# Memory added in three parts, a minimum moved behind an eviction, and one memory piece a slot, in a two-branch attention kernel

## The chip, the cores and the metric

The kernel runs on one core of a Trainium2 chip. The metric is the device time of one execution in microseconds (us). The core's engines work side by side, each through its own queue in order: TensorE (PE) multiplies, VectorE (DVE) and ScalarE (ACT) read PE's results out of PSUM, GpSimd (POOL) applies masks, and SyncE (SP) issues nearly all DMAs.

## The reference

Two independent attention layers over the same shapes (2048 tokens, 640 columns, 32 heads of 20 columns); their outputs stand side by side in the result.

```python
# A: four chunks of 512 tokens, one after the other
phi = lambda t: jnp.where(t > 0, t + 1.0, jnp.exp(t))
for s in range(4):
    logits = einsum('bhqd,bhkd->bhqk', qs, ks) * scale + mask      # inside the chunk
    a_dot = einsum('bhqk,bhkd->bhqd', softmax(logits), vs)
    pq = phi(qs)
    a_mem = einsum('bhld,bhde->bhle', pq, M) / (einsum('bhld,bhd->bhl', pq, z)[..., None] + 1e-06)
    outs.append(g * a_mem + (1.0 - g) * a_dot)
    M = M + einsum('bhld,bhle->bhde', phi(ks), vs)
    z = z + sum over l of phi(ks)
A = concat(outs) @ wo
# B: causal attention in a sliding window of 256 tokens
B = softmax(scores inside the window) @ v @ wo
```

In A, `mask` is -1e9 where the key lies behind the query's position, so each chunk is causal. The first chunk finds an empty memory.

## The kernel before

**Stages.** The work is cut into eight stages in the order B0, A0, B1, A1, B2, A2, B3, A3: a branch and one of its four chunks of 512 tokens. A stage has eight units `g` of four heads (80 columns), and its score blocks are packed so that a pack fills 384 or 512 columns of PSUM. A pack is a **slot** (`self.slot`): B0 has slots 0 to 19, A0 20 to 39, B1 40 to 63, A1 64 to 83, B2 84 to 107, A2 108 to 127, B3 128 to 151, A3 152 to 171.

**What a slot issues**, in this order on every engine's queue (`body`, from L746): steps that an earlier slot put down for its start (`self.after`: `normalise`, and `spread`, the DMAs that bring the projected q or k into the layout for scores, tiles `qp` and `kp`); the scores of the pack (`scores`: PE writes two PSUM tiles `Sc`, ACT takes each with one exponential into `pt`, L495, POOL masks `pt`); steps put down for behind the scores (`self.behind`); if a unit is due, `weigh` (PE multiplies `pt` with v into a PSUM tile `D`, DVE evicts it as `oc`, L561, SP transposes it); `prefetch` (transposed loads `oT` of finished outputs); and then dense and memory pieces as `pick` chooses them.

**PSUM.** There are three `Sc` buffers and two `D` buffers. Every dense piece, memory piece and `weigh` takes a `D`, in the order of issue, and its first matmul waits until DVE has read the `D` two before it.

**Pieces.** A projection (`proj`, L291) is five matmuls and an eviction `qk` (L294), followed by a store; a projection of v (`vproj`, L351) and half an output tile (`out_half`, L630, eviction `ot` L633) are five matmuls of 320 columns. In A1, A2 and A3 there are memory pieces: eight `read`s (L465; three DVE operations, L472, L474, L475, write a part of the tile `omem`), two halves of the columns by four token tiles, the first half first, and behind them five `upd`s (L432, DVE L442, L443), which renew the memory; A3 has no `upd`. `pick` weighs all numbers of up to three dense, three memory and three output pieces against a budget for the slot.

**Feature map.** `phi` (L317) puts down two steps for a projection of A made in slot s. `exp`, behind the scores of s+1: DVE computes max(t+1, 1) (L333) and ACT exp(t) into `pe` (L335; two buffers). `rest`, behind the scores of s+2: DVE takes the minimum of both (L338), which waits for ACT, and for k SP issues a transpose (L342).

**Outputs.** `normalise` of a unit (L590) is a reciprocal and a product on DVE (L594, L599) into its 80 columns of the tile `otA` or `otB`. In A1 and A2 the last unit's `normalise` adds all 640 columns of `omem` for four token tiles in one DVE operation (L611, 128x2560); in A3 units 4 to 7 add, unit 4 the first 400 columns.

Of the kernel before, what the change touches and what calls it, by code (L numbers as in the profile page):

```python
# [14 lines left out]
D = 640  # L15
H = 32
DH = 20
G = 8
GW = 4 * DH
KT = 5  # L20
NC = 4
# [61 lines left out]
class Kern:  # L83

    def __init__(self, ctx, tc, ins, out2d):
        self.tc, self.nc = tc, tc.nc
        self.x = {"A": ins["A_x"][0], "B": ins["B_x"][0]}
        self.ins, self.out2d = ins, out2d
        ep = ctx.enter_context
        self.cp = ep(tc.tile_pool(name="consts", bufs=1))  # L90
        self.wp = ep(tc.tile_pool(name="weights", bufs=1))
        self.io = ep(tc.tile_pool(name="io", bufs=1))
        self.wk = ep(tc.tile_pool(name="work", bufs=1))
        self.dram = ep(tc.tile_pool(name="scratch", bufs=1, space=bass.MemoryType.DRAM))
        self.ps = ep(tc.tile_pool(name="ps", bufs=1, space=bass.MemoryType.PSUM))
        self.xT, self.qp, self.kp, self.o_tok = {}, {}, {}, {}
        self.omem, self.phiq, self.mz = None, None, {}
        self.slot = 0
        self.after, self.behind = {}, {}
        self.tiles = []  # L100
        self.ready = []

# [214 lines left out]
    def phi(self, c, which, m, t, st):  # L317

        nc = self.nc
        if (which == "q" and c == 0) or (which == "k" and c == NC - 1):  # L320
            return
        if which == "q":
            if m == 0:
                self.phiq = self.io.tile([P, CT, D], BF16, name="phiq", bufs=1)[:].rearrange(
                    "p t d -> p (t d)").rearrange("p (m s) -> p m s", m=KT)
            dst = self.phiq[:, m, :]
        else:
            pk = self.wk.tile([P, CH], BF16, name="phik", bufs=3)
            dst = pk[:]
        e = self.wk.tile([P, CH], BF16, name="pe", bufs=2)  # L330

        def exp():
            nc.vector.tensor_scalar(out=dst, in0=t[:], scalar1=1.0, scalar2=1.0,  # L333
                                    op0=ALU.add, op1=ALU.max)
            nc.scalar.activation(out=e[:], in_=t[:], func=ACT.Exp)  # L335

        def rest():
            nc.vector.tensor_tensor(out=dst, in0=dst, in1=e[:], op=ALU.min)  # L338
            if which == "k":
                if m == 0:  # L340
                    st["kt"] = self.wk.tile([P, KT, CT, P], BF16, name="pkt", bufs=1)
                nc.sync.dma_start_transpose(out=st["kt"][:, m, :, :], in_=pk[:])  # L342

        self.at_end(self.slot + 1, exp)
        self.at_end(self.slot + 2, rest)

    def vproj(self, br, c, tt, hf):
        nc = self.nc
# [241 lines left out]
    def normalise(self, u, tp):  # L590
# [7 lines left out]
        cols = slice(GW * u.g, GW * (u.g + 1))  # L598
# [2 lines left out]
                                in1=rr[:].unsqueeze(3).to_broadcast([P, CT, 4, DH]),  # L601
                                op=ALU.mult)
        if u.br == "A" and u.c > 0:
            if u.c < NC - 1:
                cols = slice(0, D if u.g == G - 1 else 0)
            elif u.g < G - 4:
                cols = slice(0, 0)
            elif u.g == G - 4:
                cols = slice(0, GW * (u.g + 1))
            if cols.stop > cols.start:  # L610
                nc.vector.tensor_tensor(out=o[:, :, cols], in0=o[:, :, cols],  # L611
                                        in1=self.omem[:, :, cols], op=ALU.add)
# [115 lines left out]
    def body(self):  # L728
# [4 lines left out]
        for n, ph in enumerate(phases):  # L733
            dense = lists[n]
            mem = []
            if ph.br == "A" and ph.c > 0:
                mem = [(0.4, lambda tt=tt, hf=hf: self.read(ph.c, tt, hf))
                       for hf in range(2) for tt in range(CT)] + upd[ph.c]
            outs = 2 * OUT_TILES[n]
# [5 lines left out]
            at = [0, 0, 0]  # L745
            for i, pk in enumerate(ph.packs):  # L746
# [15 lines left out]
                if self.ready and self.ready[0][0] <= self.slot:  # L762
                    self.weigh(self.ready.pop(0)[1])
                    done += 0.75
                if outs or i >= np_ - 3:
                    self.prefetch()
                part = sum(weights[:i + 1]) / sum(weights)
                can = 2 * sum(1 for t in self.turned if t[0] + 2 <= self.slot) + len(self.half)
# [5 lines left out]
                if due > room:  # L774
                    room, can = due, 0
                for kind in self.pick(part, room, dense[at[0]:at[0] + 3],
                                      mem[at[1]:at[1] + 3], min(outs - at[2], can, 3),
                                      at, (len(dense), len(mem), outs)):
                    if kind == 2:
                        done += 0.75  # L780
                        self.out_step()
                    else:
                        a = (dense, mem)[kind][at[kind]]
                        done += a[0]
                        a[1]()
                    at[kind] += 1
# [5 lines left out]
    def pick(self, part, room, dense, mem, outs, at, total):  # L792

        best = None
        for d in range(len(dense) + 1):
            for m in range(len(mem) + 1):
                for o in range(outs + 1):
                    cost = sum(a[0] for a in dense[:d] + mem[:m]) + 0.75 * o
                    off = abs(room - cost)
# [9 lines left out]
    def tail(self, br, c):  # L809
# [9 lines left out]
                                    op=ALU.mult)  # L819
        while self.turned or self.half:  # L820
            self.out_step()
        while self.after or self.behind:
            for f in self.after.pop(self.slot, []) + self.behind.pop(self.slot, []):
                f()
            self.slot += 1
        ps[0] = self.last_sc(0)
        self.last_mm(br, 0, 0, 3)
# [63 lines left out]
```

## Time and profile before

| | us |
|---|---|
| median of three runs | 381.29 |
| lowest and highest run | 380.61 and 384.25 |
| the profiled execution, whole | 378.70 |
| its span, first to last instruction | 376.8 |
| ACT busy in the span | 339.0 |
| PE busy in the span | 335.4 |
| POOL busy in the span | 253.1 |
| DVE busy in the span | 273.0 |

The profile is of one execution. In its rows "x" gives a number of instructions, and a bracket "[2.10 <-PE ...]" the idle time of the engine before the instruction and what ended it. A stretch in which ACT has no idle time runs at ACT's pace, whatever the other engines wait for in it.

### The profile page before, as it was taken

To read this page: it belongs to the slowest core of one execution; us is meant where nothing else is said; L and a number is where in the kernel's file an instruction comes from. 1 tells how busy PE (TensorE), PEld (TensorE's weight loads), DVE (VectorE), ACT (ScalarE), POOL (GpSimd) and SP (SyncE) were. 2 spreads that over 40 slices of the span, in tenths; PEclk is the share of its full clock that TensorE was granted. 3 is DMA by queue.
4 is the path that set the end of the run, shared out by engine and by line. 5 is a ranking of instruction groups with operands and counts; after the bars stand their busy time and mean duration, and the time that the engine had idled before them with its cause. 6 is when DMAs were issued, how large, how long until landed. Compare 5 with 4: busy or idle time off the path is not lost.

```text
span 376.8 us, 10338 instructions
## 1 busy us (share of the span) xinstructions
PE 335.4 (89%) x3930; PEld 159.9 (42%) x3930; DVE 273.0 (72%) x578; ACT 339.0 (90%) x385; POOL 253.1 (67%) x392
## 2 busy tenths in 40 slices
PE   7998898999887889899987898988999989998985
PEld 3433433433443334444433344444444435444443
DVE  2465776566887687888777885787877787778783
ACT  2678899999887999899997999988999999999982
POOL 9576685555784788455587888734568988955550
PEclk9999999999999999999998999999999999999999
DMA  8964466686454847729765949825765477544622
GB/s 253 314 220 131 115 155 149 123 209 144 117 119 125 177 115 136 204 79 132 110 154 144 154 115 134 168 72 119 127 117 123 108 157 134 120 100 98 116 69 71
DMA packets 112241, 52.07 MB, mean 138 GB/s; under 512 B 81856, under 2 KB 112192, under 8 KB 112192
## 3 DMA queue, kind: packets, MB, share of 16 engines
q1 hardware_dynamic: 112048, 51.33, 60.9%
q8 instruction: 31, 0.51, 0.6%
q14 instruction: 18, 0.15, 0.1%
q10 hardware_dynamic: 144, 0.08, 0.1%
HBM read 17.05 MB, written 15.07 MB: 85 GB/s over the span
## 4 chain that ended last, share of the span: by engine, by line
PE 42%; ACT 24%; DVE 18%; issue 7%; DMA 5%; POOL 2%; SPq 1%; ACTq 0%; DVEq 0%; POOLq 0%
ACT pt L495 22%; PE D L291 14%; PE Sc L489 7%; PE D L351 6%; PE D L544 4%; PE D L630 4%; DVE qk L294 4%; DVE oc L561 2%; PE D L253 2%; ACT pe L335 2%; DMA qpB<-qdB 2%; DVE omem L475 2%; PE D L273 2%; DMA ocT<-oc 2%; DMA omem<-in_B_x_dram 1%
## 5 line engine op out<-in xcount | busy, mean ns | idle before, releaser
L495 ACT ACTIVATE pt<-Sc 128x1024 bf16<-128x1024 f32 (+1 forms) x344 | 320.7, 1068 | 22.1 <-PE Sc L489 21.4
L509 POOL TENSOR_SCALAR_AFFINE_SELECT pt<-pt 128x512 bf16<-128x512 bf16 x254 | 168.5, 674 | 107.1 <-ACT pt L495 106.6
L515 POOL TENSOR_SCALAR_AFFINE_SELECT pt<-pt 128x512 bf16<-128x512 bf16 x112 | 79.0, 719 | 4.2 <-ACT pt L495 3.5
L294 DVE CAST qk<-D 128x512 bf16<-128x512 f32 x70 | 48.1, 688 | 30.4 <-PE D L291 28.9
L489 PE MATMUL Sc<-qpB,kpB 20*128 20x256 bf16 (+2 forms) x704 | 45.0, 277 | 7.6 <-ACT pt L495 5.9
L489 PE MATMUL Sc<-qpA,kpA 20*128 20x384 bf16 (+3 forms) x512 | 39.3, 300 | 4.0 <-ACT pt L495 3.7
L561 DVE CAST oc<-D 128x512 bf16<-128x512 f32 x46 | 31.6, 688 | 14.1 <-PE D L544 13.9
L630 PEld LDWEIGHTS <-oT 128*128 128x128 bf16 x280 | 25.1, 97 | 17.4 <-issue 6.3
L489 PEld LDWEIGHTS <-kpB 20*128 20x128 bf16 x704 | 14.2, 92 | 42.8 <-issue 41.3
L633 DVE CAST ot<-D 128x320 bf16<-128x320 f32 x56 | 26.8, 485 | 5.5 <-PE D L630 4.7
L291 PE MATMUL D<-xTA,Aq 128*128 128x512 bf16 x100 | 24.9, 380 | 5.1 <-DVE oc L561 4.2
L351 PE MATMUL D<-Av,xTA 128*128 128x320 bf16 x160 | 26.3, 300 | 2.5 <-DVE vA L359 1.8
L351 PE MATMUL D<-Bv,xTB 128*128 128x320 bf16 x160 | 25.6, 300 | 2.7 <-DVE phiq L576 2.1
L291 PE MATMUL D<-xTA,Ak 128*128 128x512 bf16 x100 | 26.1, 393 | 2.0 <-DVE qk L294 2.0
L544 PE MATMUL D<-pt,vB 128*32 128x384 bf16 (+2 forms) x720 | 26.3, 277 | 1.1 <-DVE ot L633 0.5
L630 PE MATMUL D<-Bo,oT 128*128 128x320 bf16 x160 | 26.3, 300 | 0.5 <-DVE omem L475 0.3
L544 PE MATMUL D<-pt,vA 128*32 128x256 bf16 (+3 forms) x576 | 23.6, 287 | 3.3 <-DVE qk L294 2.1
L489 PEld LDWEIGHTS <-kpA 20*128 20x128 bf16 x512 | 11.5, 91 | 28.0 <-issue 25.3
L630 PE MATMUL D<-Ao,oT 128*128 128x320 bf16 x120 | 20.2, 300 | 1.0 <-DVE omem L475 0.6
L359 DVE TENSOR_TENSOR vA<-D,omg 128x320 bf16<-128x320 f32 x32 | 15.2, 485 | 6.4 <-PE D L351 6.0
L291 PE MATMUL D<-xTB,Bk 128*128 128x512 bf16 x75 | 18.8, 381 | 1.2 <-DVE omem L475 0.8
L335 ACT ACTIVATE pe<-qk 128x512 bf16<-128x512 bf16 x30 | 19.5, 659 | 0.0
(102 smaller groups left out, 363.6 us busy)
## 6 DMA issues: line engine op xcount, KB each, us to landing
out_dram<-ot SPq DMA_DIRECT2D x31, 160.0 KB
kdA<-qk SPq DMA_DIRECT2D x20, 128.0 KB
qdA<-qk SPq DMA_DIRECT2D x20, 128.0 KB
kdB<-qk SPq DMA_DIRECT2D x17, 128.0 KB
qdB<-qk SPq DMA_DIRECT2D x17, 128.0 KB
kpB<-kdB SPq DMA_DIRECT2D x8, 160.0 KB
qpB<-qdB SPq DMA_DIRECT2D x8, 160.0 KB
kpA<-kdA SPq DMA_DIRECT2D x8, 160.0 KB
```

The lines of the kernel that those rows point to most:

```text
L291: nc.tensor.matmul(ps[:], lhsT=self.w[br + which][:, kt, m * P:(m + 1) * P], rhs=self.xT[br][:, kt, :], start=(kt == 0), stop=(kt == KT - 1))
L294: nc.vector.tensor_copy(out=t[:], in_=ps[:])
L335: nc.scalar.activation(out=e[:], in_=t[:], func=ACT.Exp)
L351: nc.tensor.matmul(ps[:, 0:320], lhsT=self.xT[br][:, kt, tt * P:(tt + 1) * P], rhs=self.w[br + "v"][:, kt, hf * 320:(hf + 1) * 320], start ...
L489: nc.tensor.matmul(ps[j // 2][:, j % 2, off * P:(off + nq) * P], lhsT=kp[rows, u.g, k0:k0 + P], rhs=self.qp[u.br][rows, u.g, q0 * P:(q0 + ...
L495: nc.scalar.activation(out=pt[:, 2 * hp:2 * hp + 2, 0:pk.used], in_=ps[hp][:, :, 0:pk.used], func=ACT.Exp, scale=SCALE)
L509: nc.gpsimd.affine_select(out=blk, in_=blk, pattern=[[0, 4], [1, P]], compare_op=ALU.is_ge, fill=0.0, base=0, channel_multiplier=-1)
L515: nc.gpsimd.affine_select(out=blk, in_=blk, pattern=[[0, 4], [-1, P]], compare_op=ALU.is_ge, fill=0.0, base=-1, channel_multiplier=1)
L544: nc.tensor.matmul(O[32 * j:32 * j + 32, q0 * P:(q0 + nq) * P], lhsT=v[:, kt % CT, v0:v0 + 32], rhs=pt[:, j, off * P:(off + nq) * P], star ...
L561: nc.vector.tensor_copy(out=oc[:], in_=O[:])
L630: nc.tensor.matmul(ps[:, 0:320], lhsT=st["oT"][:, m, :], rhs=self.w[br + "o"][:, m, hf * 320:(hf + 1) * 320], start=(m == 0), stop=(m == K ...
L633: nc.vector.tensor_copy(out=st["ot"][:, hf * 320:(hf + 1) * 320], in_=ps[:, 0:320])
```

## The change

Three edits. The minimum of the feature map (`rest`) goes into a list of its own, `last_of`, which is issued in the same slot s+2 but behind `weigh`; in a slot without a due unit it stands where it stood. In A1 and A2 the memory's part is added by the units 3 (320 columns), 5 (160) and 7 (160) in place of 640 columns by unit 7; A3 is as before. And `pick` is offered one memory piece and must take it as long as there is one, so that each slot of A1, A2 and A3 issues exactly one until they are used up; the dense and output pieces are then chosen around it.

```diff
-        self.at_end(self.slot + 2, rest)
+        self.last_of.setdefault(self.slot + 2, []).append(rest)
...
         if u.br == "A" and u.c > 0:
-            if u.c < NC - 1:
-                cols = slice(0, D if u.g == G - 1 else 0)
-            elif u.g < G - 4:
-                cols = slice(0, 0)
-            elif u.g == G - 4:
-                cols = slice(0, GW * (u.g + 1))
+            c0 = {3: 0, 5: 4, 7: 6}.get(u.g, u.g + 1)
+            if u.c == NC - 1:
+                c0 = 0 if u.g == G - 4 else u.g if u.g > G - 4 else u.g + 1
+            cols = slice(GW * c0, GW * (u.g + 1))
             if cols.stop > cols.start:
...
                     self.weigh(self.ready.pop(0)[1])
                     done += 0.75
+                for f in self.last_of.pop(self.slot, []):
+                    f()
...
-                                      mem[at[1]:at[1] + 3], min(outs - at[2], can, 3),
+                                      mem[at[1]:at[1] + 1], min(outs - at[2], can, 3),
...
         for d in range(len(dense) + 1):
-            for m in range(len(mem) + 1):
+            for m in [len(mem)]:
                 for o in range(outs + 1):
```

By the two programs, the numbers of instructions of each kind stay as they are but for four more additions on DVE. In A1 the last two q projections both fall into slot 77 (before: slots 76 and 77, the last of them first in slot 77), one half output tile moves from slot 83 to 73, and one v projection out of slot 78. In A2 the last two q projections both fall into slot 121 (before: 120 and 121), and a half output tile moves from slot 125 to 117. In A3 the eight reads fall into slots 152 to 159 (before: 152 to 163). Outside of these three stages the pieces of every slot are the same.

More of the change, by code (lines that the diff above doesn't have):

```diff
@@ L98, in __init__ @@
         self.slot = 0
[L99 removed]
+        self.after, self.behind, self.last_of = {}, {}, {}
         self.tiles = []
@@ L821, in tail @@
             self.out_step()
-        while self.after or self.behind:
-            for f in self.after.pop(self.slot, []) + self.behind.pop(self.slot, []):
-                f()
+        while self.after or self.behind or self.last_of:
+            for q in (self.after, self.behind, self.last_of):
+                for f in q.pop(self.slot, []):
+                    f()
             self.slot += 1
```

## The prediction

> **What bounds the kernel now.** I read the page's busy times first, then the stages as windows, then the waits, and last the timelines of the places where ACT stands still.
>
> ```profile
> PE 335.4 (89%) x3930; PEld 159.9 (42%) x3930; DVE 273.0 (72%) x578; ACT 339.0 (90%) x385; POOL 253.1 (67%) x392
> ACT pt L495 <- PE Sc L489: 21.4, 32, 2.1
> 55.10:92.90 37.80, 35.35 (x376) 14.61 (x375) 24.18 (x48) 37.80 (x43) 21.21 (x32) 1.00 0.68 155
> 92.90:147.60 54.70, 46.69 (x558) 22.93 (x557) 43.57 (x91) 49.97 (x59) 41.54 (x64) 1.00 0.54 132
> 147.60:187.60 40.00, 36.19 (x441) 18.00 (x440) 31.88 (x77) 37.80 (x41) 21.76 (x33) 1.00 0.70 130
> 187.60:239.60 52.00, 45.49 (x529) 20.86 (x529) 39.76 (x77) 49.46 (x59) 43.30 (x64) 0.97 0.71 138
> 239.60:281.00 41.40, 37.45 (x452) 18.85 (x451) 32.38 (x80) 37.56 (x42) 21.26 (x33) 1.00 0.62 123
> 328.40:365.90 37.50, 33.68 (x426) 17.49 (x427) 29.43 (x70) 37.02 (x41) 22.68 (x35) 1.00 0.44 100
> ```
>
> In a window row come the length, then the busy time of PE, weight loads, DVE, ACT and POOL, and the granted clock. The rows are A0, B1, A1, B2, A2 and A3. A0 runs without a gap in ACT: 37.80 us for 20 slots, 1.89 each. That is what the stages cost when ACT is never kept waiting, so an edit can win only what is idle in ACT's column: 4.73 in B1, 2.20 in A1, 2.54 in B2, 3.84 in A2, 0.48 in A3. The row of the waits says that ACT's exponentials waited 21.4 us for scores in all; PE brings them late, since it waits for a PSUM buffer `D` that DVE hasn't read yet. Each edit reorders DVE, so I look for what stands on DVE ahead of each late eviction.
>
> **Part 1, the addition.** B2's gap is nearly all one place, slots 89 to 91. The rows are DVE, PE, then ACT, and last the clock in a window of 3.4 us:
>
> ```profile
> 198.63 1.80 DVE L611 TENSOR_TENSOR otA<-otA,omem 128x2560 bf16<-128x2560 bf16 x1
> 200.36 0.84 DVE L338 TENSOR_TENSOR phik<-phik,pe 128x512 bf16<-128x512 bf16 x1
> 201.13 0.68 DVE L294 CAST qk<-D 128x512 bf16<-128x512 f32 x1
> 201.86 2.26 PE L291 MATMUL D<-xTA,Ak 128*128 128x512 bf16 x5 [2.01 <-DVE qk L294]
> 204.05 0.61 PE L489 MATMUL Sc<-qpB,kpB 20*128 20x384 bf16 x8
> 201.91 0.75 ACT L335 ACTIVATE pe<-qk 128x512 bf16<-128x512 bf16 x1
> 204.76 1.94 ACT L495 ACTIVATE pt<-Sc 128x1024 bf16<-128x1024 f32 x2 [2.10 <-PE Sc L489]
> 201.90:205.30 3.40, 3.40 (x25) 1.05 (x28) 1.67 (x5) 1.30 (x3) 2.78 (x5) 0.50 0.55 128
> L611 DVE TENSOR_TENSOR otA<-otA,omem 128x320 bf16<-128x320 bf16 x3 | 1.3, 428 | 0.1
> L611 DVE TENSOR_TENSOR otA<-otA,omem 128x1600 bf16<-128x1600 bf16 x1 | 1.0, 992 | 0.0
> ```
>
> The addition of 1.80 holds back a minimum and an eviction; PE idles 2.01, its next projection takes 2.26 at a granted clock of 0.50, and ACT idles 2.10. Afterwards unit 7 adds 640 elements a partition. On the line through the two forms (0.43 at 320, 0.99 at 1600) that is 0.57, so DVE is 1.2 ahead: the projection starts at 200.65. If the half clock goes with the long wait, it takes about 1.25 and the scores start near 201.85. ACT is busy until 201.91 + 0.75 = 202.66 anyway, so the whole **2.10** is won. If the half clock stays, the scores start at 202.84 and ACT, 0.71 behind as in the rows, at 203.55: 1.2 won.
>
> The Trainium skill (TensorE: Matmul & The Clock Gate, Part 1) puts the half clock behind at least one idle window of about 3.4 us, which speaks for the second figure. The trace disagrees: 0.50 follows an idle time of 2.01. By the page's rule the gain here would be 1.2 and the sum below 0.9 smaller.
>
> In A2 the same addition stands ahead of the first of the rows below. That gap is 0.58, below the 1.2 by which DVE is ahead: **0.55** won.
>
> ```profile
> 294.66 5.67 ACT L495 ACTIVATE pt<-Sc 128x1024 bf16<-128x1024 f32 x6 [0.58 <-PE Sc L489]
> 272.53 0.49 DVE L357 CAST vB<-D 128x320 bf16<-128x320 f32 x1
> 273.44 0.73 PE L544 MATMUL D<-pt,vA 128*32 128x256 bf16 x20
> ```
>
> What moves forward costs something. Unit 3 adds 1280 elements (0.85 on the line) in slots 79 and 123, which hold two v projections each. In slot 123 it pushes the eviction at 272.53 to 273.4, done 273.9; the `weigh` at 273.44 needs that buffer, so PE loses 0.5. ACT has no gap here and PE leads it by little: **-0.45** (from 0 to -0.7). In slot 79 a loss of that size lies in front of a larger one (part 3) and isn't counted again. Unit 5's 0.57 falls into slots 84 and 128, each with a single projection behind it: DVE's free time covers it; without that cover it would be 0.5 each.
>
> **Part 2, the minimum.** It matters where a unit is due in slot s+2 and ACT waits. That is B1's start, slots 47 and 50 (DVE, PE, ACT):
>
> ```profile
> 109.38 0.85 DVE L338 TENSOR_TENSOR phik<-phik,pe 128x512 bf16<-128x512 bf16 x1
> 110.15 0.68 DVE L561 CAST oc<-D 128x512 bf16<-128x512 f32 x1
> 116.13 0.49 DVE L338 TENSOR_TENSOR phiq<-phiq,pe 128x512 bf16<-128x512 bf16 x1 [0.69 <-ACT pe L335]
> 116.65 0.74 DVE L338 TENSOR_TENSOR phik<-phik,pe 128x512 bf16<-128x512 bf16 x1
> 117.31 0.72 DVE L333 TENSOR_SCALAR phiq<-qk 128x512 bf16<-128x512 bf16 x1
> 117.95 0.67 DVE L561 CAST oc<-D 128x512 bf16<-128x512 f32 x1
> 110.88 1.24 PE L291 MATMUL D<-xTA,Aq 128*128 128x512 bf16 x5 [0.91 <-DVE oc L561]
> 115.81 1.25 PE L291 MATMUL D<-xTA,Ak 128*128 128x512 bf16 x5
> 118.68 1.24 PE L291 MATMUL D<-xTA,Aq 128*128 128x512 bf16 x5 [1.61 <-DVE oc L561]
> 113.64 1.94 ACT L495 ACTIVATE pt<-Sc 128x1024 bf16<-128x1024 f32 x2 [1.62 <-PE Sc L489]
> 116.50 1.94 ACT L495 ACTIVATE pt<-Sc 128x1024 bf16<-128x1024 f32 x2
> 118.31 0.65 ACT L335 ACTIVATE pe<-qk 128x512 bf16<-128x512 bf16 x1
> 120.34 1.94 ACT L495 ACTIVATE pt<-Sc 128x1024 bf16<-128x1024 f32 x2 [1.38 <-PE Sc L489]
> ```
>
> In slot 47 the eviction `oc` moves ahead of a minimum of 0.85: PE's projection starts about 0.7 earlier. The output eviction behind it now stands behind the minimum, so the next projection gains only 0.5; the gap of 1.62 shrinks to 1.1. In slot 50 DVE idles 0.69 for ACT and then does two minima and L333 ahead of `oc`, while the unit's matmuls are done by 115.81. Afterwards L333 (0.72) and `oc` (0.67) go first: `oc` is done near 116.9, PE goes on at 117.06 instead of 118.68, and the 1.38 falls to some 0.2. Together 3.00 of gaps become 1.3: **1.7** (from 0.7, slot 47's half and a rest, to 2.5).
>
> A new wait comes with it: the exponential at 118.31 overwrites the `pe` buffer that the first minimum of slot 50 reads, and that minimum now waits for `oc`. Behind it on ACT's queue stand the exponentials of slot 51. The minimum would be done at 117.4, ACT arrives at 117.9 or later (113.64 less 0.5): it costs nothing, with 0.5 in hand. The other slots with a minimum and a unit lie where ACT has no gap to give: nothing. On SP's queue, k's transpose falls behind the unit's; what reads it comes slots later.
>
> **Part 3, one piece a slot.** The sum of the pieces is the same; only their places change. A `read` holds DVE for about 0.95: 0.49 for the product, 0.25 for the reciprocal, and a smaller first operation. Two in one slot make PE wait, but the two that A1 and A2 now part land in slots where a projection and an eviction wait in their place. In slot 65, for one, a unit and one read stand where a unit and two reads stood; PE is through 0.9 earlier, and then loses it in slots 67 and 68 to evictions that DVE hasn't come to. Going through A1 and A2 in this way, slot by slot with the durations of these rows, the scores of slots 69 and 122 come out within 0.2 of where they are. I take nothing for the pacing, with bounds of +3 (half of A1's and A2's 6.04) and -1.5 (A1's additional half output tile and as much again of waits).
>
> ```profile
> L475 DVE TENSOR_TENSOR omem<-D,rm 128x320 bf16<-128x320 f32 x24 | 11.8, 491 | 0.8
> L474 DVE RECIPROCAL rm<-rm 128x16 f32<-128x16 f32 x24 | 6.1, 253 | 0.8
> 174.26 1.24 PE L291 MATMUL D<-xTB,Bq 128*128 128x512 bf16 x5 [0.19 <-DVE qk L294]
> 179.15 1.59 SPq L315 DMA_DIRECT2D qpB<-qdB  x4
> 187.24 0.37 PE L489 MATMUL Sc<-qpB,kpB 20*128 20x384 bf16 x5 [0.24 <-DMA qpB<-qdB]
> ```
>
> One consequence is plain, though. The last q projection of A1 (174.26) becomes the second in slot 77, and ends about 1.0 later. Its store must land before the loads at 179.15 go out, and B2's first scores wait for the last of these already (0.24 at 187.24). So slot 84 starts late: **-0.9** (from 0 to -1.5). In A2 the last q projection also becomes second, but its loads show no such wait, so I charge nothing. In A3 eight reads in eight slots load DVE more densely than before; of the 0.48 that ACT idles there little can go, and I put **-0.2** (from +0.4 to -0.6).
>
> **Sum.** 2.10 + 0.55 + 1.7 - 0.45 - 0.9 - 0.2 = 2.8. The profiled execution, 378.70, becomes 375.9. The median of the runs lies 2.6 above it, for which no row gives a reason; I carry the difference over: 381.29 - 2.8 = **378.5**.
>
> **The rivals.**
> - *The pacing pays as well.* For it: A1 and A2 idle 6.04 in ACT, much of it around slots with two reads. Against: DVE is busy for 80% of A1 and has as much to do as before. With half of it won, and slot 84 not late: 2.8 + 3 + 0.9 = 6.7, 374.6.
> - *The waits only move.* ACT and PE are both near 90% busy, so a gap closed at one place opens at the next, where PE has no lead. If the half clock stays, only slot 47's 0.5 is won at B1's start, and the rest is as above, 1.2 + 0.55 + 0.5 - 0.45 - 0.9 - 0.2 = 0.7 remains: 380.6. That the third edit does next to nothing, since the old choice issued hardly more than a piece a slot, fits this too.
> - *Slower: the late loads.* The loads of q land late for B2 by more than the projection's 1.0, because the transposes of the outputs share the DMA engines, and in A2 the same begins to show. The mechanism decides from the point where both together hold slots 84 and 128 up by more than 3.7, the other terms' sum without it. With 3 at each, 381.29 + 6 - 3.7 = 383.6. For it: the wait at 187.24; against: in A2 there is none.
>
> **How the numbers follow.** The forecast has 0.55, the pacing 0.17, the waits that move 0.21, the slower case 0.07. A range for eight in ten reaches from 375.5 to 381.2: the unknowns of the forecast alone (half clock, slot 79 and 123, slots 47 to 50) make 377.0 to 380.2, the two near rivals the rest, less the last part of the first. A measurement of this kernel can tell about 1%, 3.8 us, from no change: faster than that means below 377.5. The pacing rival gives that, and a share of the forecast's better half: 0.28. Slower than 385.1 needs more than the slower case's 383.6: 0.05. The rest, 0.67, is within 1%.
>
> **What would show it.** Right: L611 as 128x1280 and 128x640, no half clock near 200, PE's wait there below 1.0; `oc` ahead of the minimum in slots 47 and 50 and ACT's gaps there 1.1 and 0.2; a wait for `qpB<-qdB` of about 1 us at slot 84. Wrong: half clock at another place, ACT waiting at `pe` for DVE, A1's window more than 1 us shorter or longer than 40.9 to slot 84's start, or a gap of ACT in A3 above 1 us.

## The result, and the profile after

The kernel after took **379.24 us** (median of 16 runs, 377.39 to 386.39), the kernel before, on the same chip, 382.97 (16 runs, 380.29 to 386.87). The ratio is 0.9912 [0.9885, 0.9938]. In a second comparison, below, it was 0.9963 [0.9928, 0.9997]. Medians are over all runs; the ratios, and the fit further down, leave out the runs more than 1.5% above the fastest of their kernel. The change is a gain of under 1%, as forecast, but a good part of it came by a way that the forecast doesn't have.

The profiled execution took 378.26 us with a span of 376.2; before it was 378.70 and 376.8. So the two profiles differ by 0.4 us where the medians differ by 3.7. That is the first thing to explain. The page's busy times, the waits for scores and the windows of the kernel after, here cut at the first exponential of each stage (B1, A1, B2, A2, A3), with the columns as in the prediction (the last two, the DMAs' share and GB/s, are not used):

```profile
PE 332.3 (88%) x3891; PEld 160.1 (43%) x3930; DVE 273.2 (73%) x582; ACT 338.0 (90%) x385; POOL 249.7 (66%) x392
```

```profile
ACT pt L495 <- PE Sc L489: 21.1, 25, 1.5
```

```profile
94.23:146.85 52.62, 46.30 (x552) 22.91 (x556) 43.41 (x91) 50.00 (x59) 41.58 (x64) 1.00 0.57 137
146.85:187.59 40.74, 36.12 (x435) 18.41 (x441) 32.37 (x79) 36.99 (x41) 21.50 (x33) 1.00 0.79 140
187.59:236.69 49.10, 44.25 (x521) 20.75 (x526) 38.94 (x79) 49.10 (x59) 41.82 (x64) 1.00 0.71 139
236.69:279.59 42.90, 37.05 (x445) 18.88 (x450) 34.75 (x81) 37.44 (x42) 21.51 (x34) 1.00 0.60 118
326.40:364.82 38.42, 31.68 (x418) 16.70 (x415) 28.80 (x71) 37.39 (x41) 22.05 (x36) 1.00 0.43 98
```

The busy times are close to those of before: PE's are 3.1 less (fewer matmuls at half clock, and some records missing), POOL's 3.4 and ACT's 1.0. ACT still waits 21 us for scores, now 25 times in place of 32. In B2 ACT is busy 49.10 of 49.10: no gap is left there. In A2 it idles 5.46 of 42.90, where it idled 3.84 before.

The stages' lengths, from one stage's first exponential to the next one's (for A3 to the end of its last), each worked out from the starts in ACT's timeline of the profiled execution (us):

| | B0 | A0 | B1 | A1 | B2 | A2 | B3 | A3 |
|---|---|---|---|---|---|---|---|---|
| before | 44.10 | 37.55 | 54.71 | 40.11 | 51.88 | 41.32 | 47.44 | 37.53 |
| after | 45.42 | 37.55 | 52.62 | 40.74 | 49.10 | 42.90 | 46.81 | 38.43 |
| difference | +1.32 | 0 | -2.09 | +0.63 | -2.78 | +1.58 | -0.63 | +0.90 |

B1 and B2 won 4.9 us, B3 0.6, and B0, A1, A2 and A3 gave 4.4 back; the time ahead of the first and behind the last exponential is 0.4 longer. The gains are at the places that the prediction names. The start of B1, slots 47 and 50, in the timeline of the kernel after (DVE, PE, ACT):

```profile
110.74 0.68 DVE L561 CAST oc<-D 128x512 bf16<-128x512 f32 x1
111.34 0.41 DVE L338 TENSOR_TENSOR phik<-phik,pe 128x512 bf16<-128x512 bf16 x1
...
116.52 0.69 DVE L561 CAST oc<-D 128x512 bf16<-128x512 f32 x1 [0.16 <-PE D L544]
117.13 0.67 DVE L338 TENSOR_TENSOR phiq<-phiq,pe 128x512 bf16<-128x512 bf16 x1
117.49 1.24 PE L291 MATMUL D<-xTA,Aq 128*128 128x512 bf16 x5
114.23 1.94 ACT L495 ACTIVATE pt<-Sc 128x1024 bf16<-128x1024 f32 x2 [0.85 <-PE Sc L489]
118.91 0.65 ACT L335 ACTIVATE pe<-qk 128x512 bf16<-128x512 bf16 x1
119.43 1.95 ACT L495 ACTIVATE pt<-Sc 128x1024 bf16<-128x1024 f32 x2
```

`oc` now stands ahead of the minimum both times. Slot 49's gap fell from 1.62 to 0.85, slot 51's from 1.38 to nothing. PE goes on at 117.49 without idle time.

And slots 89 to 91 of B2, where the long addition was:

```profile
198.25 0.84 DVE L609 TENSOR_TENSOR otA<-otA,omem 128x640 bf16<-128x640 bf16 x1
199.01 0.85 DVE L338 TENSOR_TENSOR phik<-phik,pe 128x512 bf16<-128x512 bf16 x1
199.78 0.68 DVE L294 CAST qk<-D 128x512 bf16<-128x512 f32 x1
200.51 1.24 PE L291 MATMUL D<-xTA,Ak 128*128 128x512 bf16 x5 [0.66 <-DVE qk L294]
202.31 2.19 ACT L495 ACTIVATE pt<-Sc 128x1024 bf16<-128x1024 f32 x2
```

PE waits 0.66 in place of 2.01, its projection takes 1.24 in place of 2.26, and ACT doesn't wait at all.

What the profile shows, then, is 4.9 us won in B1 and B2 and nearly as much given back, with a span 0.6 shorter. What the medians show is a gain of 3.7. The experiments ask which edit does which of this, and what the runs have that the profiles lack.

### The profile page after: what moved, and what is told of

Its sections match the earlier page's. It is cut to its first block, busy times and chain, and to the rows that moved or that the text cites. A ratio compares the mean times of both kernels' runs of the same rounds, so it can differ in the third digit from the quotient of the medians.

```text
span 376.2 us, 10287 instructions
## 1 busy us (share of the span) xinstructions
PE 332.3 (88%) x3891; PEld 160.1 (43%) x3930; DVE 273.2 (73%) x582; ACT 338.0 (90%) x385; POOL 249.7 (66%) x392
## 4 chain that ended last, share of the span: by engine, by line
PE 37%; ACT 26%; DVE 20%; DMA 7%; issue 6%; SPq 1%; POOL 1%; ACTq 0%; DVEq 0%; POOLq 0%
ACT pt L495 23%; PE D L291 11%; PE Sc L489 7%; PE D L351 5%; DVE qk L294 4%; PE D L628 4%; PE D L544 4%; DMA ocT<-oc 3%; DVE oc L561 3%; ACT pe L335 2%; PE D L253 2%; DVE otA L599 2%; PE D L273 2%; DVE omem L475 1%; DVE otB L599 1%
## 5 line engine op out<-in xcount | busy, mean ns | idle before, releaser
L509 POOL TENSOR_SCALAR_AFFINE_SELECT pt<-pt 128x512 bf16<-128x512 bf16 x254 | 169.0, 676 | 110.8 <-ACT pt L495 110.2
L515 POOL TENSOR_SCALAR_AFFINE_SELECT pt<-pt 128x512 bf16<-128x512 bf16 x112 | 75.1, 684 | 2.8 <-ACT pt L495 2.4
L489 PE MATMUL Sc<-qpB,kpB 20*128 20x256 bf16 (+2 forms) x704 | 46.6, 275 | 10.0 <-ACT pt L495 7.8
L544 PE MATMUL D<-pt,vA 128*32 128x256 bf16 (+3 forms) x576 | 23.8, 287 | 6.2 <-DVE qk L294 2.9
L544 PE MATMUL D<-pt,vB 128*32 128x384 bf16 (+2 forms) x720 | 25.9, 275 | 1.1 <-DVE ot L631 0.5
L291 PE MATMUL D<-xTA,Ak 128*128 128x512 bf16 x87 | 24.2, 381 | 1.4 <-DVE qk L294 0.7
L335 ACT ACTIVATE pe<-qk 128x512 bf16<-128x512 bf16 x30 | 22.0, 738 | 0.0
L544 PEld LDWEIGHTS <-vA 128*32 128x32 bf16 x576 | 12.8, 96 | 17.0 <-DVE qk L294 5.4
```

The lines of the kernel that those rows point to most:

```text
L291: nc.tensor.matmul(ps[:], lhsT=self.w[br + which][:, kt, m * P:(m + 1) * P], rhs=self.xT[br][:, kt, :], start=(kt == 0), stop=(kt == KT - 1))
L489: nc.tensor.matmul(ps[j // 2][:, j % 2, off * P:(off + nq) * P], lhsT=kp[rows, u.g, k0:k0 + P], rhs=self.qp[u.br][rows, u.g, q0 * P:(q0 + ...
L509: nc.gpsimd.affine_select(out=blk, in_=blk, pattern=[[0, 4], [1, P]], compare_op=ALU.is_ge, fill=0.0, base=0, channel_multiplier=-1)
L515: nc.gpsimd.affine_select(out=blk, in_=blk, pattern=[[0, 4], [-1, P]], compare_op=ALU.is_ge, fill=0.0, base=-1, channel_multiplier=1)
L544: nc.tensor.matmul(O[32 * j:32 * j + 32, q0 * P:(q0 + nq) * P], lhsT=v[:, kt % CT, v0:v0 + 32], rhs=pt[:, j, off * P:(off + nq) * P], star ...
```

## The experiments

### The three edits one by one, and the first two together

The addition in three parts alone:

```diff
-            if u.c < NC - 1:
-                cols = slice(0, D if u.g == G - 1 else 0)
...
+            c0 = {3: 0, 5: 4, 7: 6}.get(u.g, u.g + 1)
...
```

> Edit 1 alone (the addition in three parts). Forecast theory: the gaps of ACT at slots 91 (2.10) and 135 (0.58) go, slot 125 gains a gap of about 0.45, the rest of the profile stays as before: B2 about 2.7 us shorter, B3 0.6 shorter, A2 0.5 longer, time 2.2 us below the kernel before (ratio 0.994). Theory of the clock: what the median of the runs loses is half-clock windows behind PE's wait at slot 89, so this edit alone takes most of the whole change's gain in the median (ratio about 0.991 or below) and the runs show fewer windows. Theory that the waits only move: below 1 us (0.998).

The minimum behind the eviction alone:

```diff
-        self.at_end(self.slot + 2, rest)
+        self.last_of.setdefault(self.slot + 2, []).append(rest)
...
```

> Edit 2 alone (the minimum behind the eviction of the sums). Forecast theory: B1's gaps at slots 49 and 51 go from 3.00 to about 1.0 and nothing else changes, so B0 is as long as before; time 1.7 to 2.1 us below (ratio 0.995). Theory of the queue: the transposes that change places on SP's queue in slots 11 and 19 make the loads of B0's last unit late, so B0 is about 1.3 us longer with gaps at slots 17 and 18, as in the profile after, and the time falls by less than 1 us (0.998).

One memory piece a slot alone:

```diff
-                                      mem[at[1]:at[1] + 3], min(outs - at[2], can, 3),
+                                      mem[at[1]:at[1] + 1], min(outs - at[2], can, 3),
...
-            for m in range(len(mem) + 1):
+            for m in [len(mem)]:
```

> Edit 3 alone (one memory piece a slot). Forecast theory: A1 to the start of slot 84 0.9 us longer, A2 unchanged, A3 0.2 longer, time 1.1 us above (ratio 1.003). Theory that the pacing is what the profile after shows as losses: A1 to slot 84 0.6 longer, A2 1.1 longer (1.6 less the addition's 0.45), A3 0.9 longer, time 2.6 us above (1.007). Theory that the pacing pays: time 1 us or more below.

The addition and the minimum, without the pacing:

```diff
+            c0 = {3: 0, 5: 4, 7: 6}.get(u.g, u.g + 1)
...
+        self.last_of.setdefault(self.slot + 2, []).append(rest)
...
```

> Edits 1 and 2 without 3. If the terms add up as in the forecast: 2.2 and 1.7 to 2.1, about 4 us below before (ratio 0.9895), and 1 us or more below the whole change. If the pacing is what the losses in A1, A2 and A3 of the profile after come from, 2.5 us below the whole change (0.985). If the pacing pays, above the whole change's 0.991.

Measured (the kernel before, beside all four: 382.2 us, 35 runs; stages in us from the profiled executions):

| | median us | ratio | B0 | B1 | A1 | B2 | A2 | B3 | A3 |
|---|---|---|---|---|---|---|---|---|---|
| before | 382.2 | 1 | 44.10 | 54.71 | 40.11 | 51.88 | 41.32 | 47.44 | 37.53 |
| addition | 382.34 | 1.004 [0.9996, 1.0084] | 44.10 | 54.71 | 40.71 | 50.82 | 42.57 | 47.45 | 37.41 |
| minimum | 378.52 | 0.9901 [0.9863, 0.994] | 44.30 | 54.14 | 39.77 | 51.76 | 41.37 | 47.28 | 37.53 |
| pacing | 383.40 | 1.005 [1.0012, 1.0088] | 44.10 | 54.71 | 40.71 | 50.78 | 41.88 | 48.11 | 39.17 |
| addition, minimum | 378.42 | 0.9911 [0.9876, 0.9946] | 44.31 | 52.62 | 40.69 | 49.71 | 42.56 | 46.81 | 37.53 |

The minimum is the whole gain. The addition alone wins nothing, the pacing alone loses half a per cent, and the first two together give what the minimum gives alone. Where an edit doesn't touch a stage, most lengths agree to 0.01 us from one kernel to another (A0 has 37.55 in all of them, B1 54.71 in three). Two things disturb this. TensorE at half clock makes a stage longer: the profiles have such a window in the B2 of before, in the B1 and the B2 of the minimum and in the A3 of the pacing, and in no other stage of the table. And A1 varies by itself: in eight profiles of kernels with the same work in it, it has 39.64 to 40.42, though ACT's gaps inside it agree to 0.2; a wait at slot 84, which counts as A1's, makes up to 0.5 of this.

The addition loses in A1 (a new gap of 0.81 at slot 81) and in A2 (+1.25). What it wins in B2 is less than the table's 1.06, or 2.05 on top of the minimum. The pacing has the long addition in its B2 and takes 50.78 there, as little as the addition's 50.82. PE and ACT at this place with the pacing alone, then two windows of 3.41 us of the same profile, and the window of before that holds PE's wait:

```profile
202.77 1.24 PE L291 MATMUL D<-xTA,Ak 128*128 128x512 bf16 x5 [2.01 <-DVE qk L294]
204.43 1.94 ACT L495 ACTIVATE pt<-Sc 128x1024 bf16<-128x1024 f32 x2 [0.86 <-PE Sc L489]
198.59:202.00 3.41, 2.17 (x18) 1.07 (x17) 3.34 (x5) 3.41 (x6) 3.11 (x4) 1.00 0.54 108
202.00:205.41 3.41, 2.64 (x40) 1.25 (x40) 2.71 (x7) 2.55 (x5) 3.41 (x6) 1.00 0.39 95
198.51:201.92 3.41, 1.40 (x15) 0.75 (x14) 3.38 (x5) 3.41 (x5) 3.41 (x4) 1.00 0.56 135
```

PE waits the same 2.01 behind the same addition, but what follows has full clock, and ACT's gap is 0.86, not 2.10. (The kernel of the next part shows the same three numbers: 2.01, full clock, 0.86.) So some 1.2 of the 2.10 was the half clock's. Clock aside, the addition alone only moves B2's gaps: 0.34 is left at slot 91, and slot 106 has 1.01 in place of 0.35. On top of the minimum it wins between 0.2 and 0.9: with 1.1 for the half clock taken off the minimum's 51.76 (an estimate, from before and the pacing) 50.6 would be left, and a kernel below, which keeps the long addition and has no half clock in B2, takes 49.87, against 49.71 here. The two windows ahead differ in this: in before the wait lies within one of them, with PE busy for 41% of it; with the pacing it lies across the end of one with 64%.

The loss of A2, in the timeline of the kernel with the first two edits, slots 122 to 125 (DVE, PE, ACT):

```profile
270.06 1.14 DVE L609 TENSOR_TENSOR otA<-otA,omem 128x1280 bf16<-128x1280 bf16 x1
271.13 0.87 DVE L357 CAST vB<-D 128x320 bf16<-128x320 f32 x2
271.66 0.73 PE L544 MATMUL D<-pt,vA 128*32 128x256 bf16 x20 [1.20 <-DVE vB L357]
273.62 1.94 ACT L495 ACTIVATE pt<-Sc 128x1024 bf16<-128x1024 f32 x2 [1.03 <-PE Sc L489]
```

This is the place that the prediction priced at 0.45: the addition of unit 3 stands ahead of the eviction of a v projection. It takes 1.14, not 0.85, PE waits 1.20 for it, not 0.5, and ACT, which had no gap here, gets one of 1.03. In A1, slot 81, the same cost 0.81. Nor were the additions of 640 elements as short as I had put them: 0.80 to 0.84, not 0.57.

The traces show what the prediction's line had mixed. Its 0.43 at 320 elements is the mean of 0.64, 0.33 and 0.32. These additions of A3 in the kernel before, with POOL's masks at that time, and then the two additions of 1280 in the kernel after, with the masks beside them:

```profile
360.18 0.99 DVE L611 TENSOR_TENSOR otA<-otA,omem 128x1600 bf16<-128x1600 bf16 x1
362.77 0.64 DVE L611 TENSOR_TENSOR otA<-otA,omem 128x320 bf16<-128x320 bf16 x1
367.19 0.33 DVE L611 TENSOR_TENSOR otA<-otA,omem 128x320 bf16<-128x320 bf16 x1
360.49 3.41 POOL L509 TENSOR_SCALAR_AFFINE_SELECT pt<-pt 128x512 bf16<-128x512 bf16 x4 [1.20 <-ACT pt L495]
```

```profile
178.72 0.82 DVE L609 TENSOR_TENSOR otA<-otA,omem 128x1280 bf16<-128x1280 bf16 x1
178.77 1.86 POOL L509 TENSOR_SCALAR_AFFINE_SELECT pt<-pt 128x512 bf16<-128x512 bf16 x2 [1.98 <-ACT pt L495]
270.57 1.14 DVE L609 TENSOR_TENSOR otA<-otA,omem 128x1280 bf16<-128x1280 bf16 x1
269.56 1.47 POOL L509 TENSOR_SCALAR_AFFINE_SELECT pt<-pt 128x512 bf16<-128x512 bf16 x2 [2.01 <-ACT pt L495]
```

The additions at 362.77 and 270.57 begin while POOL is at a mask; those at 360.18, 367.19 and 178.72 begin while it is idle. All 106 such additions in the 14 profiles divide in this way. The 60 that begin during a mask take 0.64 at 320 elements, 0.80 to 0.84 at 640, 1.14 at 1280, 1.47 at 1920 and 1.80 to 1.85 at 2560; the other 46 take 0.32 at 320, 0.82 at 1280 and 0.99 at 1600. Each group lies on a line, and the first line is 0.31 above the second. No run moved a mask away from an addition, so that the mask is the cause is read from the traces and not tested.

What the pacing costs in A1, in the timeline of the kernel after (DVE, PE, ACT, slots 72 to 74):

```profile
165.02 0.68 DVE L294 CAST qk<-D 128x512 bf16<-128x512 f32 x1
165.62 0.29 DVE L442 TENSOR_TENSOR macc<-D,macc 128x147 f32<-128x147 f32 x1
165.95 0.32 DVE L443 TENSOR_TENSOR mz<-macc,bmask 128x147 bf16<-128x147 f32 x1
165.75 0.73 PE L544 MATMUL D<-pt,vA 128*32 128x512 bf16 x16 [0.70 <-DVE qk L294]
167.27 0.84 PE L628 MATMUL D<-Bo,oT 128*128 128x320 bf16 x5 [0.42 <-DVE oc L561]
168.58 7.44 ACT L495 ACTIVATE pt<-Sc 128x1024 bf16<-128x1024 f32 x8 [1.50 <-PE Sc L489]
```

Every slot now carries a `read` or an update of the memory (L442, L443) beside its projection and its unit, and PE waits 0.70 and 0.42 in one slot. The 1.50 that ACT idles, where it idled 0.24 before, stands in the profile of the pacing alone, too:

```profile
169.48 7.44 ACT L495 ACTIVATE pt<-Sc 128x1024 bf16<-128x1024 f32 x8 [1.50 <-PE Sc L489]
```

In A3 the eight reads in eight slots cost 0.9 (38.43 against 37.53 without the edit), by a gap of 0.73 at slot 157, where the kernel before has none, in the timeline of the kernel after:

```profile
332.44 0.38 PE L465 MATMUL D<-mz,phiq 128*128 128x147 bf16 x5 [0.70 <-DVE omem L475]
336.78 3.77 ACT L495 ACTIVATE pt<-Sc 128x1024 bf16<-128x1024 f32 x4 [0.73 <-PE Sc L489]
```

The longer A3 of the pacing alone, 39.17, has half-clock time in it as well, which the next part takes up. In the pacing's B3, 0.67 longer with the same pieces, 0.35 is a gap at slot 150; what made it is open.

### Is it the "one" or the "must" of the pacing?

The kernel before, with at most one memory piece offered to a slot, but none forced:

```diff
-                                      mem[at[1]:at[1] + 3], min(outs - at[2], can, 3),
+                                      mem[at[1]:at[1] + 1], min(outs - at[2], can, 3),
```

> Half of edit 3 alone: at most one memory piece a slot, but none is forced, so that a dense piece can go first. If it is the forced piece that costs time in A1, A2 and A3 (reads taken while DVE is behind): shorter than with edit 3 alone by 1 us or more, ratio 0.998 to 1.001. If the cap itself does (the pieces end later, dense work comes in lumps): as edit 3 alone, 1.005, or worse. If two pieces in a slot were what made PE wait: below 0.996.

Measured: 381.75 us beside 381.0, ratio 1.0015 [0.9981, 1.0048]: no change. A1 is 40.33 (before 40.11) and A2 41.34 (41.32), and ACT's gaps in them come to 2.44 and 2.74, against 1.99 and 3.80 before and 3.75 and 4.69 with the pacing alone. So, as far as one profile of each shows, the costs of the pacing in these two stages go with the forced piece. In A3 ACT has no gap at slots 156 and 157 here.

This profile showed something else. Two windows of it, at B1's and A3's places:

```profile
127.57:130.98 3.41, 3.41 (x15) 1.31 (x11) 0.69 (x1) 2.59 (x3) 2.91 (x6) 0.50 0.92 173
342.60:346.01 3.41, 3.41 (x36) 1.44 (x25) 1.80 (x4) 1.79 (x3) 1.42 (x3) 0.50 0.38 75
```

Both run wholly at a granted clock of 0.50 with PE busy throughout. B1 took 55.86, not 54.71, and A3 38.70, not 37.53, while the orders of their work had hardly changed: +1.15 and +1.17. A third such window, at 236.8, lies in its B2 (52.81).

### How many half-clock windows does a run have?

Every profile of every kernel here shows the half clock, if at all, in windows of 3.41 us at 0.50, which lie on a grid of that length. Each run lists its mean granted clock, so the number of windows in it can be worked out: (1 - clock) x span / 1.7, as a window at 0.50 is worth half of 3.41. I did that for 201 runs of the eleven kernels (the record has no clock for the kernel before in the first comparison, so its runs there are not among them), and fitted the time to the number of windows, with one common slope and a level for each kernel. One window costs **1.28 us** of the run (95%: +-0.10). Over all 228 runs with a clock on record the slope is 1.46 (+-0.09), so 1.3 to 1.5 is what can be said. The stages above fit this: B2 of before is 1.10 longer than the pacing's, and the two of the last part were 1.15 and 1.17 longer.

| | windows a run, mean | time at no window, us | runs |
|---|---|---|---|
| before | 2.64 | 377.9 | 75 |
| after | 1.54 | 377.6 | 26 |
| addition | 1.99 | 379.5 | 11 |
| minimum | 2.23 | 375.4 | 21 |
| pacing | 2.22 | 380.4 | 11 |
| addition, minimum | 1.16 | 377.1 | 12 |

The times at no window are good to 0.3 (before) to 0.5 us. The kernel with one memory piece at most has 2.76 windows and 378.4. The profile of before had one window, the profile of after none. So the 2.6 us by which the median of before lay above its profiled execution is mostly this: 1.64 windows more, at 1.28, are 2.1. And the gain of the whole change, in the means of these runs 1.6 us, is 1.4 us by 1.1 windows fewer a run, and only 0.2 in the time at no window, which the fit can't tell from nothing. Within the second comparison alone, below, the means differ by 1.5: 1.0 by 0.8 windows, and 0.5. Clock aside, the minimum wins 2.5, the addition alone loses 1.6, and the pacing alone 2.5.

### The whole change once more

No edit; the kernel after again, beside the best of the variants below.

> The whole change once more, for its profile. If B0's 1.3 us (gaps at slots 17 and 18 in the profile after) comes from the transposes that changed places on SP's queue, it is here again (B0 45.4). If it was one late DMA issue of that execution, B0 is as with edit 2 alone, 44.3, and the span 1 us shorter. A1, A2 and A3 as in the profile after (40.7, 42.9, 38.4). Ratio 0.991, about 1.6 half-clock windows a run.

Measured: 380.11 us (12 runs, 377.34 to 381.95) beside 381.78 (23 runs), ratio 0.9963 [0.9928, 0.9997]. The stages are those of the first profile to 0.1, but for B0 (44.93), A1 (41.14) and B2 (49.60). There is a half-clock window at 365.6, nearly all of it behind the last exponential. The two intervals meet only between 0.9928 and 0.9938: some 0.7% are won, less than the first comparison alone says.

### Where should the addition go?

If the loss is unit 3's addition ahead of a v projection's eviction, later units should avoid it. The first two edits, with units 5 (480 columns) and 7 (160):

```diff
-            c0 = {3: 0, 5: 4, 7: 6}.get(u.g, u.g + 1)
+            c0 = {5: 0, 7: 6}.get(u.g, u.g + 1)
```

> Edits 1 and 2 without 3, but the addition in two parts, by units 5 (480 columns) and 7 (160), so that nothing is added in slots 79 and 123. Theory that the parts moved forward cost what edit 1 wins: the gaps of ACT at slots 81 (0.81) and 125 (1.03) of the run with edits 1 and 2 go, A1 is about 0.9 and A2 about 1.2 us shorter than there, slot 86 or 87 gains at most 0.3, time about 2 us below that run (ratio to before 0.986). Theory that DVE has no free time anywhere: the gap only moves to slots 85 to 87, the time stays at 0.991.

The same with units 5 (480 columns), 6 and 7 (80 each):

```diff
-            c0 = {3: 0, 5: 4, 7: 6}.get(u.g, u.g + 1)
+            c0 = {5: 0, 6: 6, 7: 7}.get(u.g, u.g + 1)
```

> As the one before, but three parts, by units 5 (480 columns), 6 and 7 (80 each): the addition ahead of the projection's eviction in slots 89 and 133 is half as long. Theory of the moved parts: like the one before within 0.5 us (0.986). If slot 89's wait still counts after its cut to 640 elements, 0.5 us or more below it, with fewer half-clock windows in the runs.

The second edit alone, with no addition at all in A1 and A2. The memory's part is then missing from the outputs of the second and the third chunk; the time is that of the kernel without this work:

```diff
-                cols = slice(0, D if u.g == G - 1 else 0)
+                cols = slice(0, 0)
```

> Edit 2 alone, and the addition of the memory's part left out altogether in A1 and A2 (the output lacks it there): the most that any place for the addition could win beside edit 2. Theory of the clock: PE's wait in slot 89 is gone, so a run has about 1.5 half-clock windows fewer than with edit 2 alone (2.6 on average), at 1.4 to 1.7 us each, and B2 is 1 to 2 us shorter even without them; A1 and A2 as with edit 2: ratio 0.980 to 0.983. If the windows do not hang on that wait: about 2.5 of them still, ratio 0.986.

And the variant with units 5, 6 and 7 in a second comparison, beside the whole change:

> Edits 1 and 2 with the addition by units 5 (480 columns), 6 and 7, once more beside the whole change on one chip. By its first run 376.8, ratio 0.9885, 0.8 half-clock windows a run; A1, A2, A3 39.7, 41.4, 37.5. If the pacing and the early parts of the addition are what the change gives away, 2 us or more below the whole change in the same job (ratio 0.986); if the first run was luck, within 1 us of it.

Measured (the kernel before: 381.0 beside the first three, 381.78 beside the last):

| | median us | ratio | A1 | B2 | A2 | B3 | windows a run |
|---|---|---|---|---|---|---|---|
| units 5, 7 | 378.85 | 0.9898 [0.9837, 0.996] | 39.93 | 51.08 | 41.36 | 47.39 | 1.05 |
| units 5, 6, 7 | 376.81 | 0.9885 [0.983, 0.994] | 39.72 | 49.42 | 41.37 | 47.39 | 0.85 |
| no addition | 376.51 | 0.9873 [0.9803, 0.9942] | 40.42 | 48.87 | 41.36 | 46.70 | 1.06 |
| units 5, 6, 7, again | 377.39 | 0.9907 [0.987, 0.9944] | 39.79 | 49.78 | 41.37 | 47.40 | 1.44 |

Both variants have A2 back at 41.4, so the loss there was unit 3's place. With units 5, 6 and 7 B2 stays short (49.42 and 49.78), and the spans are 371.8 and 372.8, 2.8 and 1.8 below that of the first two edits with the units 3, 5 and 7. What is left to win from this operation isn't settled: by the medians the kernel without the addition is 0.3 us faster, by the spans 0.2 to 1.3, and by the times at no window 1.3 (374.7, good to 0.7, against 376.0, good to 0.4). In the same comparison the variant is 2.7 us below the whole change (377.39 and 380.11). Among the versions with the right output it has one of the two lowest medians; the kernel with five matmuls that nothing needs, below, has the other (376.76), and the runs don't tell the two apart.

### Does PE's idle time bring on the half clock?

Two kernels tell whether the windows follow from how long PE waits. One is the minimum alone again, with the long addition and its wait of PE in slot 90:

> Edit 2 alone again, beside the one with the filled wait. By its first run 2.6 half-clock windows a run, ratio 0.990, B1 52.6 where no half clock falls into it, A1 39.8, A2 41.4, A3 37.5. If the first was luck of the chip: above 0.993.

The other is the same kernel with five matmuls that nothing needs in that wait, into the second scores tile of slot 90, which its own scores overwrite:

```diff
+                if self.slot == 90 and j == 2 and off == 0:
+                    for i in range(5):
+                        nc.tensor.matmul(ps[1][:, i % 2, :], lhsT=self.ident[:],
+                                         rhs=self.w["Bk"][:, i, 0:CH], start=True, stop=True)
```

> Edit 2 alone, with five additional matmuls of 128x512 in slot 90 (into the second scores tile, before its scores overwrite it; the output is the same). They fill about 1.1 us of PE's wait of 2.0 for the eviction behind the long addition; ACT needs the tile only later. Nothing else moves, and nothing of the wait itself goes. Theory that the half clock follows PE's idle share of a window: about one window a run fewer than with edit 2 alone in the same job, and 1.5 us less. Theory that it hangs on the wait's cause or on something else: as many windows, and the same time or up to 0.3 us more.

Measured in one comparison (the kernel before: 381.61): the minimum alone 378.17, 0.9932 [0.9891, 0.9973]; with the five matmuls 376.76, 0.9887 [0.9833, 0.994]. First PE's timeline and the windows of the minimum alone, around slots 90 and 91:

```profile
201.27 1.28 PE L291 MATMUL D<-xTA,Ak 128*128 128x512 bf16 x5 [2.50 <-DVE qk L294]
203.02 1.47 PE L544 MATMUL D<-pt,vB 128*32 128x384 bf16 x24
```

```profile
198.93:202.34 3.41, 1.07 (x5) 0.38 (x4) 2.91 (x5) 2.77 (x4) 3.41 (x5) 1.00 0.55 112
202.34:205.75 3.41, 3.41 (x38) 1.40 (x37) 2.06 (x4) 2.46 (x3) 1.67 (x3) 0.50 0.49 131
```

Then the same two views with the five matmuls in it (L490; the lines behind it are moved by four, so L548 is the former L544):

```profile
198.29 1.25 PE L490 MATMUL Sc<-Bk,ident 128*128 128x512 bf16 x5
200.24 1.24 PE L291 MATMUL D<-xTA,Ak 128*128 128x512 bf16 x5 [0.37 <-DVE qk L294]
201.74 0.84 PE L548 MATMUL D<-pt,vB 128*32 128x384 bf16 x24
```

```profile
197.00:200.40 3.40, 3.03 (x21) 1.29 (x20) 3.40 (x4) 2.52 (x4) 3.40 (x4) 1.00 0.62 156
200.40:203.80 3.40, 3.40 (x51) 1.55 (x50) 2.66 (x6) 3.40 (x5) 2.71 (x5) 1.00 0.55 128
```

A window with PE busy 1.07 of 3.41 is followed by one at half clock, in which the `weigh` takes 1.47; with the matmuls PE is busy 3.03, the next window has the full clock, and the `weigh` takes 0.84. The order of the work and the long addition (1.84 here) are the same otherwise. Over the runs the filler has 1.28 windows (from 1.1 to 2.2) in place of 2.3 (from 1.1 to 4.0), and both kernels come to the same 375.4 at no window. So more work on PE made the kernel 1.4 us faster by medians. Three reservations: the two ratios' intervals overlap; in the profile of the filler the five matmuls stand ahead of slot 90's own scores, and ACT idles 0.88 there; and in the same profile a DMA for which DVE had waited 0.54 ahead of the addition came in time, so that a part of PE's shorter wait isn't the filler's. Nor does every such wait bring half clock: the pacing's profile, above, has the wait of 2.01 across two windows and full clock behind it.

## Why the prediction was right, and where it was not

The time, the range and "within 1%" held: 379.24 against 378.5, with a difference of 3.7 against the 2.8 of the sum (1.7 in the second comparison). The terms behind it fared as follows.

- **The minimum: right.** 1.7 was set for B1's start; B1 became 2.09 shorter. (In the profile of the minimum alone a half-clock window in B1 hides most of this: 54.14.) Of the two gaps, slot 49's closed more than I had it (0.85, not 1.1) and slot 51's wholly. ACT's new wait at `pe` cost nothing, as foreseen. Where "nothing" was set for the other slots, slot 13's gap in B0 fell and slot 18's rose, with +0.2 in all.
- **The addition in B2: mis-sized, since most of its 2.10 was the clock's.** In the whole change's profile the gap of 2.10 closed and no half clock came, as forecast. But two profiles with the long addition and the same wait of 2.01, the pacing's and that with one piece at most, have full clock and a gap of 0.86. So the wait itself cost 0.86, and the other 1.2 is a half-clock window, which this place has in some profiles and not in others; the term should have had a chance in it. Alone the addition won nothing in B2 that the clock doesn't explain (50.82 against 50.78), since the gap at slot 106 grew from 0.35 to 1.01; it needed the minimum's edit beside it. The half clock came without the idle window that the Trainium skill's rule, weighed in the prediction, asks for (TensorE: Matmul & The Clock Gate, Part 1): PE was busy for 41% of the window ahead of it. The 0.55 of A2's end came likewise only with both edits (B3's length 46.81, and 47.45 with the addition alone).
- **The addition's moved part: the step that failed most.** Set at -0.45 for slot 123, it was 1.25 in A2; and the loss in slot 79, which "isn't counted again", was a gap of 0.81 at slot 81. The durations came from a line through two forms of A3 (0.57 and 0.85; measured 0.81 and up to 1.14), and that line went from additions of which one began during a mask of POOL to one that didn't. With 1.14 in place of 0.85 PE lost 1.20, not 0.5, and nearly all of it reached ACT (1.03): that PE leads ACT by little there was right.
- **The pacing: wrong.** I took nothing for it, -0.9 for the loads of q at slot 84 and -0.2 for A3. No wait for `qpB` shows at slot 84: ACT had lost the time before, in slots 68, 69, 74 and 78, to evictions behind reads. By itself the edit makes A1 0.6 and A2 0.56 longer, and A3 0.9 on top of the others. On top of the other two it costs about 0.5 clock aside (377.6 against 377.1), less than the levels' uncertainty.
- **The carried difference: the step that hid this.** I wrote that for the 2.6 us between median and profiled execution "no row gives a reason". The rows with 0.50 were the reason: the profile had one window, the runs 2.64. With 1.1 fewer windows after, that difference shrank by 1.4, which I had no term for, and this made up for the addition's and the pacing's costs. The sum was right in part by two errors that cancel.
- **The rivals.** "The waits only move" describes A1, A2 and A3 well, where 3.1 of the 4.9 that B1 and B2 won were lost again, though its premise, that the half clock stays, did not come. Its time, 380.6, is as near to the two medians (379.24 and 380.11) as the forecast's. The pacing did not pay, and the late loads didn't come.

One part of the profiles has no cause that I can name: B0 took 1.1 more in the profile of after than with the first two edits alone. On SP's queue one group of loads took longer there; first the kernel after, then the kernel before, in SP's timeline:

```profile
45.47 2.47 SPq L315 DMA_DIRECT2D qpB<-qdB  x4
```

```profile
44.91 1.45 SPq L315 DMA_DIRECT2D qpB<-qdB  x4
```

The four issues took 1.0 longer, and the scores of slot 17 waited for what they load. In the second profile of the same kernel B0 is 44.93. Both lengths are above the 44.27 to 44.36 of the eight profiles that have the minimum's edit without the pacing, though the pacing changes nothing in B0's order of work; it stays open what it is.

## What to carry to other kernels

An operation that is moved is paid for at its new place: look there at how far PE is ahead of ACT, and take its duration from rows in which the other engines do the same beside it: here an addition that began during a mask of GpSimd took 0.31 us longer. Where the median lies above the profiled execution, look for what that execution had less of before you carry the difference over; here it was windows at half clock, whose number the mean granted clock of each run gives. And a long wait of TensorE costs twice where it is followed by half clock, which it was in some profiles here and not in others, so splitting the work that it waits for, or filling the wait, can win although ACT's gap there is small. Before a gap is called an edit's gain, look at the granted clock there on both sides.

## What the runs showed of the hardware

- **Half clock after short waits.** The Trainium skill (TensorE: Matmul & The Clock Gate, Part 1) has TensorE slow down behind at least one idle window of about 3.4 us. The traces agree on the length (3.41) and differ on the condition: PE was never idle for a whole window. In the profiles here those ahead of a half clock had PE busy for 31% to 72%, after single waits of 2.0 to 2.5 us among others, and in other places windows of 53% to 62% were followed by full clock. Between 12 and 366 us, the four windows below 50% (31%, 41%, 42%, 49%) were all followed by half clock. The same wait of 2.01 had half clock behind it where it lay within one window (41%) and full clock where it lay across two (57% and 64% in the first of them, in two profiles). One threshold in PE's busy share doesn't part these cases, since 72% had half clock behind it once.
- **The number of windows differs from run to run of one kernel**, with a mean of 1.1 to 2.8 by kernel, and each costs 1.3 to 1.5 us of a run of 380. So a median of a few runs, or one profile, can differ from another by a few us with no instruction changed.
- **One operation, two durations.** An addition of two bf16 tiles on DVE takes 0.31 us longer when it begins during a mask on POOL: 0.64 against 0.32 at 320 elements, 1.14 against 0.82 at 1280, the two sizes that occur both ways. All 106 additions in the 14 profiles go one way or the other; that the mask causes it wasn't tested by a run.
